# A linear-attention and MoE kernel: queries projected with tokens moving, and their maxima taken across partitions

## The chip, the cores and the metric

The kernel runs on one core of a Trainium2 chip. The time is device microseconds of one launch; three runs of the kernel before gave 825.32, 826.61 and 826.67 us, median 826.61.

## What is computed

```python
def phi(x):
    proj = np.einsum('bhsd,df->bhsf', x, w_phi)
    proj = proj - np.max(np.abs(proj), axis=-1, keepdims=True)
    return np.concatenate([np.exp(proj), np.exp(-proj)], axis=-1)
q_p, k_p = (phi(q), phi(k))
kv = np.einsum('bhsf,bhsd->bhfd', k_p, v)
z = np.sum(k_p, axis=2)
num = np.einsum('bhsf,bhfd->bhsd', q_p, kv)
den = np.einsum('bhsf,bhf->bhs', q_p, z)[..., None] + 1e-06
attn = num / den
```

There are 8 batches, 8 heads, 576 tokens, a head dimension of 64 and 128 features. The heads' outputs are laid side by side (512 wide) and go through h = relu(x @ w_in) (1024 wide), a convolution over three neighbouring tokens, a sigmoid gate of it on h, and a product with w_out. All is fp32 in and out.

## The kernel before, in words

**Products in parts.** Most operands are split into a high part that TensorE takes in its fp32r format and the rest, a low part, and three products (high by high, high by low, low by high) are summed. `split` (L57) does this with a copy and a subtraction. Batch 0's queries, and a few other products, are plain fp32 and take one instruction, of which the trace shows two records.

**Attention.** A unit is one batch `b` and one half `qd` of its heads, 16 units in all. Of a unit, group 0 holds 128 token columns (the last 64 tokens of two head pairs) and groups 1 to 4 hold 256 tokens of one pair. A tile's two heads lie on partitions 0 to 63 and 64 to 127. So there are 80 groups of queries, 64 large and 16 small, and as many of keys.

`load_split` (L172) loads a group by SyncE's queue and splits it on GpSimd (L62, L65). `project` (L185) makes, for each 128 tokens, a product with the tokens as the stationary operand and a block-diagonal `w_phi` of 256 columns moving: the result has tokens on partitions and features along the row (L196 in fp32, or L199 to L201). VectorE takes each row's maximum (L204) and subtracts it (L206), from PSUM to SBUF. Keys stay so. In `q_process` (L300) each 128 x 128 block of the queries is then transposed by TensorE with an identity matrix (L320, tile tp), ScalarE makes both exponentials (L326), splits them with VectorE (tile ql), and the products with kv (L348, L356, tile nm) follow. kv's own products (L255) are interleaved with them. `x_process` (L384) divides: sums go by DMA to one row (den, L392, L393, rr), VectorE multiplies (L406) and, with ScalarE, splits the result into xh and xl. xl1_3_0 is batch 1, head pair 3, half 0 of the tokens.

**MoE.** For each batch and each half of its tokens (16 parts, n = 2 b + half) `h_part` makes h (L429, tile hp), GpSimd and VectorE convolve (L452, L457, tile c), ScalarE's sigmoid gates, VectorE multiplies (L465) and splits (tile gl), and `o_part` makes the output (L488, tile op). hp2 is the first part of batch 1. `weight_process` rounds the 16 pieces of the MoE weights at the start (tiles w_t and w_r, L96 to L105), on VectorE, ScalarE and GpSimd.

**The order.** The program is written out by a planner (L513 on): each process yields estimates of TensorE's time (`pe(ns)`), delays (`wait(ns)`) and conditions (`until`), up to 13 attention processes are open at once, and attention and MoE are interleaved by their remaining shares. A scheduler then sets each engine's queue. Engines run their queues in that order. The lines around the change:

```python
pr = project(n, hi, lo, b, qd, g, "q")
yield pe(330 * n)
...
tp = pg.tile([P, 2, n, P], F32, name=f"tp{b}_{qd}_{g}", tag="g", bufs=4)
for t in range(n):
    for i in range(2):
        nc.tensor.transpose(out=tp[:, i, t, :], in_=pr[:, 2 * t + i, :], identity=idn)
```

Four PSUM buffers (tag g) serve the key and query projections, the transposes and nm.

## Time and profile before

| what | value |
|---|---|
| median of three runs | 826.61 us |
| the profiled execution | 825.6 us |
| its span, first to last instruction | 823.5 us |
| mean granted TensorE clock | 0.989 |
| busy share of ScalarE, GpSimd | 69%, 37% |
| first matmul of the MoE (hp0) | at 65.7 us |
| hp2, the MoE's first part of batch 1 | at 210.0 us |
| attention's last query group | ends near 708 us |

The profile's views give, for a group of like instructions, their count, their busy time, the mean of one, and the engine's idle time just before them with what ended it. PE is TensorE's matmuls, PEld its weight loads, DVE VectorE, ACT ScalarE, POOL GpSimd, SP SyncE. Matmuls are pipelined, so one's duration is longer than the time from its start to the next one's.

### The profile page before, as it was taken

What the parts mean: (1) busy time and instruction counts of PE and PEld (TensorE: products, weight loads), DVE (VectorE), ACT (ScalarE), POOL (GpSimd) and SP (SyncE); (2) the same over time, 40 slices, a digit from 0 to 9 for tenths busy, and PEclk for the clock granted to TensorE, in tenths of its full rate; (3) what the DMA queues carried; (4) which work ended last, traced back from release to release, by engine and by line L of the source; (5) the groups of instructions that cost most, each with busy time, mean ns of one, the idle gap of its engine ahead of it and who ended that gap; (6) DMA issues with size and microseconds to landing.
All of it is one profiled execution on the core that took longest, in us unless ns stands there. A gap on an engine that the chain in (4) does not pass through costs nothing.

```text
span 823.5 us, 17817 instructions
## 1 busy us (share of the span) xinstructions
PE 788.0 (96%) x6350; PEld 772.5 (94%) x6350; DVE 645.6 (78%) x1390; ACT 569.5 (69%) x1228; POOL 307.6 (37%) x467
## 2 busy tenths in 40 slices
PE   7778779999999999999999999999999999999998
PEld 6767678999999999999999999999999999999998
DVE  4879999799987769787779878788697878766551
ACT  4598777797788867687586857678576867644332
POOL 4757765444443424414233333424334131111110
PEclk9799989999999999999999999999999999999999
DMA  6544421211211302121121211112021100000001
GB/s 187 157 134 135 135 66 47 67 41 44 70 56 44 93 18 71 27 82 50 46 61 43 69 34 60 47 50 82 15 77 29 56 12 19 13 30 30 23 23 44
DMA packets 56328, 49.18 MB, mean 60 GB/s; under 512 B 15024, under 2 KB 54192, under 8 KB 56240
## 3 DMA queue, kind: packets, MB, share of 16 engines
q1 hardware_dynamic: 56240, 48.05, 20.1%
q8 instruction: 51, 0.84, 0.4%
q14 instruction: 37, 0.30, 0.1%
HBM read 38.13 MB, written 9.44 MB: 58 GB/s over the span
## 4 chain that ended last, share of the span: by engine, by line
PE 74%; DVE 10%; ACT 7%; issue 4%; DMA 3%; POOL 1%; SPq 1%; DVEq 0%; ACTq 0%; POOLq 0%
PE op L488 22%; PE hp L429 21%; PE kv L255 8%; PE nm L356 8%; PE tp L320 3%; PE kp L199 2%; PE nm L348 2%; PE kp L200 2%; PE kp L201 2%; PE qp L199 1%; PE qp L200 1%; PE qp L201 1%; DMA w_r<-in_w_in_dram 1%; PE kv L251 1%; DVE qm L204 1%
## 5 line engine op out<-in xcount | busy, mean ns | idle before, releaser
L457 DVE SCALAR_TENSOR_TENSOR c<-h,cw,c 128x287 f32<-128x287 f32 (+1 forms) x256 | 138.7, 554 | 49.4 <-POOL c L452 47.5
L452 POOL TENSOR_SCALAR c<-h,cw 128x288 f32<-128x288 f32 x128 | 75.0, 588 | 243.6 <-ACT h L436 184.3
L255 PE MATMUL kv<-v,ke 128*128 128x65 f32 x1024 | 159.4, 255 | 1.4 <-ACT ke L236 1.2
L255 PEld LDWEIGHTS kv<-v,ke 128*128 128x128 f32 x1024 | 153.5, 193 | 4.8 <-ACT ke L236 1.8
L429 PE MATMUL hp<-xh,win_hi 128*128 128x290 f32 x512 | 153.2, 300 | 0.6 <-ACT os L493 0.6
L429 PE MATMUL hp<-xl,win_hi 128*128 128x290 f32 x512 | 152.7, 298 | 0.2 <-DVE xl L65 0.2
L488 PE MATMUL op<-gh,wout_hi 128*128 128x288 f32 x512 | 152.2, 298 | 0.0
L429 PE MATMUL hp<-xh,win_lo 128*128 128x290 f32 x512 | 151.9, 297 | 0.0
L488 PE MATMUL op<-gl,wout_hi 128*128 128x288 f32 x512 | 151.4, 296 | 0.0
L488 PE MATMUL op<-gh,wout_lo 128*128 128x288 f32 x512 | 150.9, 295 | 0.0
L436 ACT ACTIVATE h<-hp 128x290 f32<-128x290 f32 x128 | 52.2, 414 | 71.7 <-PE hp L429 71.2
L429 PEld LDWEIGHTS hp<-xh,win_hi 128*128 128x128 f32 x512 | 96.7, 190 | 1.5 <-ACT os L493 1.4
L62 POOL TENSOR_SCALAR kxh<-kr 128x256 fp32r<-128x256 f32 (+1 forms) x80 | 43.8, 547 | 144.1 <-PE kp L200 134.6
L429 PEld LDWEIGHTS hp<-xl,win_hi 128*128 128x128 f32 x512 | 97.0, 189 | 0.6 <-DVE xl L65 0.6
L429 PEld LDWEIGHTS hp<-xh,win_lo 128*128 128x128 f32 x512 | 97.1, 190 | 0.0
L488 PEld LDWEIGHTS op<-gh,wout_lo 128*128 128x128 f32 x512 | 96.4, 188 | 0.0
L488 PEld LDWEIGHTS op<-gl,wout_hi 128*128 128x128 f32 x512 | 96.2, 188 | 0.0
L488 PEld LDWEIGHTS op<-gh,wout_hi 128*128 128x128 f32 x512 | 96.1, 188 | 0.0
L65 DVE TENSOR_TENSOR ql<-qe,qh 128x512 fp32r<-128x512 f32 x112 | 79.9, 732 | 9.9 <-ACT qh L60 9.5
L236 ACT ACTIVATE ke<-ks 128x512 f32<-128x512 f32 (+1 forms) x80 | 46.9, 586 | 39.1 <-DVE ks L206 36.5
L326 ACT ACTIVATE qe<-tp 128x512 f32<-128x512 f32 x112 | 61.2, 595 | 12.2 <-PE tp L320 10.4
L356 PE MATMUL nm<-ql,kvh 128*65 128x256 f32 x224 | 68.4, 308 | 0.3 <-DVE ql L65 0.2
(84 smaller groups left out, 1989.5 us busy)
## 6 DMA issues: line engine op xcount, KB each, us to landing
v<-in_vt_dram SPq DMA_DIRECT2D x80, 130.0 KB
out_dram<-os SPq DMA_DIRECT2D x64, 144.0 KB
qr<-in_qT_dram SPq DMA_DIRECT2D x64, 128.0 KB
kr<-in_kT_dram SPq DMA_DIRECT2D x64, 128.0 KB
w_r<-in_w_in_dram SPq DMA_DIRECT2D x8, 512.0 KB
w_r<-in_w_out_dram SPq DMA_DIRECT2D x8, 512.0 KB
rr<-rc SPq DMA_DIRECT2D x128, 2.2 KB
qr<-in_qT_dram SPq DMA_DIRECT2D x16, 64.0 KB
```

The lines of the kernel that those rows point to most:

```text
L62: nc.gpsimd.tensor_scalar(out=hi, in0=src, scalar1=1.0, scalar2=0.0, op0=ALU.mult, op1=ALU.add)
L65: eng_lo.tensor_tensor(out=lo, in0=src, in1=hi.bitcast(F32), op=ALU.subtract)
L199: nc.tensor.matmul(out=o, lhsT=his, rhs=wbd_hi, start=True, stop=False)
L236: nc.scalar.activation(out=e[:, 0], in_=pr, func=AF.Exp)
L255: ins = nc.tensor.matmul(out=kp[i][:, s, p0 : p0 + VW], lhsT=lhsT, rhs=v[:, (2 * t + i) * VW : (2 * t + i + 1) * VW], start=False, stop=(g ...
L326: nc.scalar.activation(out=e, in_=tp.rearrange("p i t s -> p i (t s)"), func=AF.Exp, scale=1.0 - 2.0 * s)
L356: ins = after(ins, lambda: nc.tensor.matmul(out=ps[:, i, o : o + w], lhsT=w_, rhs=x_, start=(k == 0), stop=(k == 5)))
L429: nc.tensor.matmul(out=ps, lhsT=w_, rhs=x_, start=(k == 0), stop=(k == 11))
L436: nc.scalar.activation(out=hs, in_=ps, func=AF.Relu)
L452: nc.gpsimd.tensor_scalar(out=cv, in0=hs[:, o : o + TC], scalar1=cw[:, f, 1:2], scalar2=0.0, op0=ALU.mult, op1=ALU.add)
L457: nc.vector.scalar_tensor_tensor(out=cv[:, lo:hi], in0=hs[:, o + j - 1 + lo : o + j - 1 + hi], scalar=cw[:, f, j : j + 1], in1=cv[:, lo:hi ...
L488: nc.tensor.matmul(out=ps, lhsT=w_, rhs=x_, start=(k == 0), stop=(k == 23))
```

## The change

The queries' projection is turned round. The weights (64 x 128, the same for both heads) are stationary and the tokens move, 512 columns for two heads of 256 tokens, so that features come out on partitions as the exponentials need them.

- Loading: the two heads lie side by side along the row, and the same data is loaded twice, to partitions 0 to 63 and 64 to 127 (two DMAs instead of one, except in batch 0). GpSimd splits the whole (a copy on 128 partitions x 512, then a subtraction on the upper 64), so that the upper half holds the low parts.
- Two matmuls of 512 columns make the projection: `wq_hi` (the high weights, in both halves) and `wq_lo` (the low weights, zero below). In batch 0 one fp32 product on 64 partitions does it.
- The maximum over features now runs across partitions. VectorE's reduce with `apply_transpose` takes it in blocks of 32 partitions x 32 columns, three copies bring the other quarters' maxima to partitions 64 to 95, and a second small reduce joins them.
- GpSimd splits the maxima in two parts (two small ops) and multiplies them with a 32 x 32 identity (`eye`) into the moving operand's upper half, which is free by then.
- A third matmul, with -1 as its weights (`wq_m`), subtracts the maximum into the same PSUM buffer, and the exponentials read that.
- The subtraction on VectorE (L206) and the transposes are gone for queries, so are the PSUM buffer tp and the 128 x 128 identity. The planner's estimates follow (`pe(230 * n)`, `pe(115 * n)`). Keys stay as they are.

```diff
+        if kind == "q":
+            f32 = 2 * b + qd < NQ_F32
+            raw = sb.tile([P, 2, n * P], F32, name=f"qr{b}_{qd}_{g}", tag="qr", bufs=2)
+            for h in range(1 if f32 else 2):
+                nc.sync.dma_start(out=raw[D * h : D * h + D, :, :],
+                                  in_=src[b, qd, :, c0 : c0 + n * P].rearrange("(i d) s -> d i s", d=D))
+            x = sb.tile([P, 2, n * P], F32R, name=f"qx{b}_{qd}_{g}", tag="qx", bufs=2)
+            if f32:
+                return n, x, raw
+            nc.gpsimd.tensor_scalar(out=x, in0=raw, scalar1=1.0, scalar2=0.0, op0=ALU.mult, op1=ALU.add)
+            nc.gpsimd.tensor_tensor(out=x[D:P], in0=raw[D:P], in1=x[D:P].bitcast(F32), op=ALU.subtract)
+            return n, x, None
...
-        pr = project(n, hi, lo, b, qd, g, "q")
-        yield pe(330 * n)
-        yield wait(1700)
+        if raw is None:
+            nc.tensor.matmul(out=tpf, lhsT=wq_hi, rhs=xf, start=True, stop=False, skip_group_check=True)
+            nc.tensor.matmul(out=tpf, lhsT=wq_lo, rhs=xf, start=False, stop=False, skip_group_check=True)
+        else:
+            nc.tensor.matmul(out=tpf, lhsT=wbd_f[0:D, 0:F], rhs=raw.rearrange("p i s -> p (i s)")[0:D], start=True, stop=False,
+                             skip_group_check=True)
+
+        c = w // 32
+        mt = sb.tile([P, 4, 16], F32, name=f"qmt{b}_{qd}_{g}", tag="qmt", bufs=2)
+        nc.vector.tensor_reduce(out=mt[:, 2, 0:c], in_=tpf.rearrange("p (c f) -> p c f", f=32), axis=AX, op=ALU.max,
+                                apply_absolute_value=True, apply_transpose=True)
+        for a in (0, 1, 3):
+            nc.vector.tensor_copy(out=mt[D : D + 32, a, 0:c], in_=mt[32 * a : 32 * a + 32, 2, 0:c])
+        m = sb.tile([P, 16], F32, name=f"qm{b}_{qd}_{g}", tag="qm", bufs=2)
+        nc.vector.tensor_reduce(out=m[D : D + 32, 0:c], in_=mt[D : D + 32, :, 0:c].rearrange("p a c -> p c a"), axis=AX, op=ALU.max)
+        mp = sb.tile([P, 16], F32R, name=f"qmp{b}_{qd}_{g}", tag="qmp", bufs=2)
+        nc.gpsimd.tensor_copy(out=mp[D : D + 32, 0:c], in_=m[D : D + 32, 0:c])
+        nc.gpsimd.tensor_tensor(out=mp[D + 32 : P, 0:c], in0=m[D : D + 32, 0:c], in1=mp[D : D + 32, 0:c].bitcast(F32),
+                                op=ALU.subtract)
+
+        nc.gpsimd.tensor_tensor(out=xf[D:P, :].rearrange("p (c t) -> p c t", t=32),
+                                in0=mp[D:P, 0:c].bitcast(F32).unsqueeze(2).broadcast_to([D, c, 32]),
+                                in1=eye[D:P, :].unsqueeze(1).broadcast_to([D, c, 32]), op=ALU.mult)
+        yield pe(230 * n)
+        yield wait(2500)
...
-        for t in range(n):
-            for i in range(2):
-                nc.tensor.transpose(out=tp[:, i, t, :], in_=pr[:, 2 * t + i, :], identity=idn)
+        r = slice(0, P) if raw is None else slice(D, P)
+        nc.tensor.matmul(out=tpf, lhsT=wq_m[r, :], rhs=xf[r, :], start=False, stop=True, skip_group_check=True)
...
-        yield pe(220 * n)
+        yield pe(115 * n)
```

The planner and the scheduler make a new order of it. Line numbers in the rows of the order of the changed kernel are its own: L335, L336 and L362 are the three matmuls, L338 the fp32 product, L343, L346 and L348 the reduce, the copies and the second reduce, L197, L198, L350, L351 and L354 GpSimd's five ops, L471 and L530 hp and op. Names carry batch, half and group, and a running number of the tile.

On TensorE, just ahead of hp2, before:

```order
L199 MATMUL qp2_1_1_2878<-wbd_hi_72,qxh2_1_1_2738 128x256
L200 MATMUL qp2_1_1_2878<-wbd_lo_73,qxh2_1_1_2738 128x256
L201 MATMUL qp2_1_1_2878<-wbd_hi_72,qxl2_1_1_2739 128x256
...
L488 MATMUL op0_3_2409<-gl0_4_2222,wout_hi7_108 128x288
L488 MATMUL op0_3_2409<-gh0_4_2221,wout_lo7_116 128x288
L429 MATMUL hp2_0_2938<-xh1_0_0_2001,win_hi0_93 128x290
```

and now:

```order
L335 MATMUL qp2_0_1_2545<-qx2_0_1_2317,wq_hi_76 128x512
L336 MATMUL qp2_0_1_2545<-qx2_0_1_2317,wq_lo_77 128x512
L530 MATMUL op0_3_2445<-gh0_4_2271,wout_lo7_126 128x288
L471 MATMUL hp2_0_2964<-xh1_0_0_2048,win_hi0_103 128x290
L471 MATMUL hp2_0_2964<-xl1_0_0_2049,win_hi0_103 128x290
```

The projections are two long matmuls instead of six, and when hp2 is reached the queries stand at group 1 of unit (2, 0), not of unit (2, 1): less attention stands ahead of it.

On VectorE, around xl1_3_0, before:

```order
L465 TENSOR_TENSOR c1_2231<-c1_2231,h1_6_2100 128x288
L465 TENSOR_TENSOR c1_2231<-c1_2231,h1_7_2115 128x288
L65 TENSOR_TENSOR xl1_3_0_2857<-xf1_3_0_2853,xh1_3_0_2856 128x290
L204 TENSOR_REDUCE km2_1_4_2812<-kp2_1_4_2805 128x4
L65 TENSOR_TENSOR xl1_3_1_2864<-xf1_3_1_2860,xh1_3_1_2863 128x290
L204 TENSOR_REDUCE qm2_1_0_2823<-qp2_1_0_2819 128x2
```

and now:

```order
L447 STREAM_SHUFFLE xf1_3_1_2920<-rr_84 128x290
L448 TENSOR_TENSOR xf1_3_0_2913<-num1_1_1_1978,xf1_3_0_2913 128x290
L448 TENSOR_TENSOR xf1_3_1_2920<-num1_1_1_1978,xf1_3_1_2920 128x290
L65 TENSOR_TENSOR ql2_0_2_2663<-qe2_0_2_0_2664,qh2_0_2_2662 128x512
L65 TENSOR_TENSOR xl1_3_0_2917<-xf1_3_0_2913,xh1_3_0_2916 128x290
L65 TENSOR_TENSOR ql2_0_2_2663<-qe2_0_2_1_2668,qh2_0_2_2662 128x512
L65 TENSOR_TENSOR xl1_3_1_2924<-xf1_3_1_2920,xh1_3_1_2923 128x290
L343 TENSOR_REDUCE qmt2_0_3_2689<-qp2_0_3_2686 128x16
L346 COPY qmt2_0_3_2689<-qmt2_0_3_2689 32x16 x3
L348 TENSOR_REDUCE qm2_0_3_2694<-qmt2_0_3_2689 32x16
```

A query group's reduce and subtraction are now a reduce, three copies and a small reduce. Ahead of xl1_3_0 stand 23 query groups, and stood 25; all 16 pieces gl of the MoE's first two parts stand ahead of it now, and 8 did.

On GpSimd, in batch 1, the changed kernel has:

```order
L350 CAST qmp1_1_2_1630<-qm1_1_2_1628 32x16
L351 TENSOR_TENSOR qmp1_1_2_1630<-qm1_1_2_1628,qmp1_1_2_1630 32x16
L354 TENSOR_TENSOR qx1_1_2_1482<-qmp1_1_2_1630,eye_81 64x512
L197 TENSOR_SCALAR qx1_1_4_1651<-qr1_1_4_1648 128x512
L198 TENSOR_TENSOR qx1_1_4_1651<-qr1_1_4_1648,qx1_1_4_1651 64x512
L494 TENSOR_SCALAR c1_2281<-h1_0_1787,cw_92 128x288
L494 TENSOR_SCALAR c1_2281<-h1_2_1817,cw_92 128x288
...
L350 CAST qmp1_1_3_1907<-qm1_1_3_1905 32x16
L494 TENSOR_SCALAR c1_2281<-h1_6_2156,cw_92 128x288
```

Where only the splits of loaded queries and keys stood between the convolution's ops, the middle step of a query group now stands there too, behind the convolution's ops that wait for h.

More of the change, by code (lines that the diff above doesn't have):

```diff
@@ L78 @@
     split(wbd_f, wbd_hi, wbd_lo, nc.vector, nc.vector)
-    idn = load_const(ident, [P, P], "idn")
+    wq_hi = cp.tile([P, F], F32R, name="wq_hi")
+    wq_lo = cp.tile([P, F], F32R, name="wq_lo")
+    wq_m = cp.tile([P, F], F32R, name="wq_m")
+    for i in range(2):
+        r = slice(D * i, D * i + D)
+        nc.vector.tensor_copy(out=wq_hi[r, :], in_=wbd_hi[r, i * F : (i + 1) * F].bitcast(F32))
+    eye = cp.tile([P, 32], F32, name="eye")
+    for p in (D, D + 32):
+        nc.sync.dma_start(out=eye[p : p + 32, :], in_=ident[p : p + 32, p : p + 32])
     rr = cp.tile([P, S], F32, name="rr")
     nc.gpsimd.memset(rr, 0.0)
+    nc.gpsimd.tensor_copy(out=wq_m, in_=rr[:, 0:F])
+    nc.gpsimd.tensor_copy(out=wq_lo, in_=rr[:, 0:F])
+    nc.vector.tensor_copy(out=wq_lo[0:D, :], in_=wbd_lo[0:D, 0:F].bitcast(F32))
+    nc.gpsimd.tensor_scalar(out=wq_m[D:P, :], in0=rr[D:P, 0:F], scalar1=-1.0, scalar2=0.0, op0=ALU.add, op1=ALU.add)
     bias_e = cp.tile([P, 1], F32, name="bias_e")
@@ L173, in load_split @@
         c0, n = group_columns(g)
-        if kind == "q" and 2 * b + qd < NQ_F32:
-            raw = sb.tile([P, n * P], F32, name=f"{kind}r{b}_{qd}_{g}", tag=kind + "xh", bufs=2)
-            nc.sync.dma_start(out=raw, in_=src[b, qd, :, c0 : c0 + n * P])
-            return n, raw, None
+        if kind == "q":
[10 more added lines that the diff above has]
+            return n, x, None
         raw = sb.tile([P, n * P], F32, name=f"{kind}r{b}_{qd}_{g}", tag=kind + "r", bufs=2)
@@ L194, in project @@
             his = hi[:, t * P : (t + 1) * P]
-            if lo is None:
-                nc.tensor.matmul(out=o, lhsT=his, rhs=wbd_f, start=True, stop=True)
-                continue
             los = lo[:, t * P : (t + 1) * P]
@@ L306, in q_process @@
         yield until(back("qp", 2))
-        n, hi, lo = load_split(qT, b, qd, g, "q")
+        n, x, raw = load_split(qT, b, qd, g, "q")
         yield wait(3000)
@@ L310, in q_process @@
         set_ready(("qp", *divmod(j, 5)))
-        pr = project(n, hi, lo, b, qd, g, "q")
-        yield pe(330 * n)
-        yield wait(1700)
+        w = n * 2 * P
+        tp = pg.tile([P, 2, n, P], F32, name=f"qp{b}_{qd}_{g}", tag="g", bufs=4)
+        tpf = tp.rearrange("p i t s -> p (i t s)")
+        xf = x.rearrange("p i s -> p (i s)")
+        if raw is None:
[4 more added lines that the diff above has]
+                             skip_group_check=True)
@@ L314, in q_process @@
+        yield pe(230 * n)
+        yield wait(2500)
         yield until(back("num", 2))
         set_ready(("tp", *divmod(j, 5)))
-        tp = pg.tile([P, 2, n, P], F32, name=f"tp{b}_{qd}_{g}", tag="g", bufs=4)
-        for t in range(n):
-            for i in range(2):
-                nc.tensor.transpose(out=tp[:, i, t, :], in_=pr[:, 2 * t + i, :], identity=idn)
+        r = slice(0, P) if raw is None else slice(D, P)
+        nc.tensor.matmul(out=tpf, lhsT=wq_m[r, :], rhs=xf[r, :], start=False, stop=True, skip_group_check=True)
```

## The prediction

> **What bounds the kernel now.** The page's busy shares come first, then the stretches, then the meeting point of two engines.
>
> ```profile
> span 823.5 us, 17817 instructions
> PE 788.0 (96%) x6350; PEld 772.5 (94%) x6350; DVE 645.6 (78%) x1390; ACT 569.5 (69%) x1228; POOL 307.6 (37%) x467
> ```
>
> TensorE looks like the bound, but that is a mean. The stretches (length, then busy time of PE, PEld, DVE, ACT, POOL) show two different kernels:
>
> ```profile
> 0.00:60.00 60.00, 45.69 (x293) 40.96 (x294) 41.43 (x76) 37.86 (x78) 34.68 (x47) 0.91 0.53 155
> 60.00:140.00 80.00, 64.88 (x497) 58.54 (x496) 78.45 (x147) 61.94 (x134) 56.61 (x66) 0.96 0.35 104
> 140.00:210.00 70.00, 68.47 (x576) 67.70 (x575) 61.54 (x136) 58.12 (x123) 31.42 (x47) 1.00 0.20 54
> 210.00:700.00 490.00, 489.65 (x4106) 487.52 (x4105) 394.63 (x869) 358.74 (x780) 168.70 (x277) 1.00 0.18 50
> 700.00:823.50 123.50, 119.29 (x888) 117.75 (x886) 69.52 (x167) 52.88 (x116) 16.20 (x32) 1.00 0.08 27
> ```
>
> From 60 to 140 us VectorE is busy 78.45 of 80 us and TensorE only 64.88: VectorE paces that part (it also converts the MoE weights there). From 140 us on TensorE is full, VectorE at 81% (394.63 of 490). The hand-over is batch 1's input to the MoE: its piece xl1_3_0 is made by VectorE here, and TensorE starts the MoE part hp2, which reads it, here.
>
> ```profile
> 206.22 0.45 DVE L65 TENSOR_TENSOR xl<-xf,xh 128x290 fp32r<-128x290 f32 x1
> 209.99 0.30 PE L429 MATMUL hp<-xh,win_hi 128*128 128x290 f32 x1
> ```
>
> Every engine runs its queue in order, so the time is: the start of hp2 (210.0), plus TensorE's work queued from there on, plus what it idles after.
>
> **TensorE's part of the change.** Matmuls overlap, so I price them from start to start:
>
> ```profile
> 208.35 0.28 PE L199 MATMUL qp<-wbd_hi,qxh 128*128 128x256 f32 x1
> 209.06 0.30 PE L488 MATMUL op<-gh,wout_lo 128*128 128x288 f32 x1
> 716.18 12.80 PE op L488 x96
> 80.80 0.60 PE L320 MATMUL tp<-idn,qs 128*128 128x128 f32 x4
> 41.77 1.56 PE L196 MATMUL qp<-wbd_f,qr 128*128 128x256 f32 x6 [1.18 <-ACT qh L326]
> 56.31 1.13 PE L196 MATMUL qp<-wbd_f,qr 128*128 128x256 f32 x4 [1.55 <-ACT qh L326]
> ```
>
> Six q projections of 256 columns lie between the first two starts: 0.71/6 = 0.118 us. 288 columns take 12.80/96 = 0.133, so 32 columns more cost 0.015 and 512 columns, which no row shows, are estimated at 0.225 (0.118 + 256 x 0.42 ns). Four transposes end 0.60 us after the first started; less one's 0.28 of latency that is 0.108 each. Two fp32 records more cost 0.43, so a 256-column fp32 product (two records) is 0.43 and a 512-column one 0.86.
>
> The Trainium skill, "TensorE: Matmul & The Clock Gate", section on 56 against 53.3 ns, states N/2.4 GHz + 2.5 ns, 215.7 ns at 512 columns. By that the 176 matmuls of 512 columns would be 1.6 us cheaper in all; its 109 ns at 256 columns is less than the 118 shown, so I stay with 0.225.
>
> A group of 256 tokens x 2 heads: before 6 x 0.118 + 4 x 0.108 = 1.14, after 3 x 0.225 = 0.675; a 128-token group 0.57 and 0.35; the ten fp32 groups of batch 0 go from 1.30 to 1.09. With 56 and 14 groups of the first kinds the cut is 26.0 + 3.0 + 1.9, about **31 us** of TensorE work. Of these, work ahead of hp2 is worth nothing by itself: at such prices the rows ahead of it fill some 155 of the 210 us.
>
> What counts stands behind hp2. Counting the rows of the order: before, 288 q matmuls (34.0) and 198 transposes (21.4) stand behind it, 55.4 us; after, 142 of 512 and 33 of 256 columns, 35.9 us: 19.5 less. But the new order runs less attention ahead: 27 k projections, 47 products nm of 256 and 8 of 64 columns, 32 + 4 kv products now stand behind hp2 and stood ahead. One nm and two kv records take 0.29 here:
>
> ```profile
> 420.64 0.33 PE L255 MATMUL kv<-v,ke 128*128 128x65 f32 x2
> 420.79 0.31 PE L356 MATMUL nm<-ql,kvh 128*65 128x256 f32 x1
> 420.93 0.33 PE L255 MATMUL kv<-v,ke 128*128 128x65 f32 x2
> ```
>
> So a kv product is 0.17 (the wider ones, and nm of 64 columns, taken in proportion, 0.22 and 0.12): 3.2 + 5.5 + 0.9 + 5.4 + 0.9 = 15.9 us come back. Behind hp2 TensorE has **about 4 us less** to do, not 31. In all there stand behind it, before: 1440 op and 1344 hp (0.133, 0.134), 1095 matmuls of 256 columns, 198 transposes, 328 + 40 kv products, 88 short nm: 597 us; after, 593.5.
>
> **VectorE up to xl1_3_0.** The rows of the first 210 us:
>
> ```profile
> L65 DVE TENSOR_TENSOR ql<-qe,qh 128x512 fp32r<-128x512 f32 x24 | 19.9, 852 | 2.0 <-ACT qh L60 2.0
> L206 DVE TENSOR_TENSOR qs<-qp,qm 128x512 f32<-128x512 f32 x20 | 13.5, 676 | 0.0
> L65 DVE TENSOR_TENSOR xl<-xf,xh 128x290 fp32r<-128x290 f32 x16 | 10.8, 682 | 0.3 <-ACT xh L60 0.3
> L406 DVE TENSOR_TENSOR xf<-num,xf 128x290 f32<-128x290 f32 x16 | 9.7, 636 | 0.0
> L65 DVE TENSOR_TENSOR gl<-c,gh 128x288 fp32r<-128x288 f32 x8 | 3.7, 512 | 0.0
> L392 DVE TENSOR_SCALAR den<-den 72x16 f32<-72x16 f32 x9 | 3.0, 337 | 3.9 <-DMA den<-dr 2.6 <-issue 1.3
> L204 DVE TENSOR_REDUCE qm<-qp 128x2 f32<-128x256 f32 x6 | 2.5, 411 | 0.0
> L392 DVE TENSOR_SCALAR den<-den x32: 156/171/1227, 52.4 to 710.7; 72x16 f32<-72x16 f32 x32
> ```
>
> Ahead of xl1_3_0 stood 25 q groups (5 of them small), each a reduce and a subtraction at 0.676 or 0.411: 31.2 us. Now 23 stand there (5 small). No row has the transposing reduce; I take the plain one's price: 18 x 0.676 + 5 x 0.411 = 14.2. The second reduce over 64 elements is estimated at 0.21 (0.676 less 448 elements at 1.04 ns, the slope between 0.411 and 0.676): 4.8. The other differences, 8 gl more, 3 ql, one k group and one den less, cancel. That is -12 us, and 69 copies of 32x16 come in. Nearest row: the 72x16 op, 0.156 at its fastest, 0.337 on average here. So the sum is **-1 to +11 us**; at 0.26, midway, +6.
>
> These copies read and write SBUF, and GpSimd is a neighbour that hurts: the same ops late in the kernel, where GpSimd is 13% busy (16.20 of 123.5) and not 58% (122.7 of 210), take
>
> ```profile
> L65 DVE TENSOR_TENSOR ql<-qe,qh 128x512 fp32r<-128x512 f32 x3 | 2.1, 688 | 1.0 <-ACT qh L60 1.0
> L65 DVE TENSOR_TENSOR xl<-xf,xh 128x290 fp32r<-128x290 f32 x8 | 3.7, 463 | 1.2 <-ACT xh L60 1.2
> ```
>
> while qs, fed from PSUM, is not stretched. The excess is 0.16 us on a ql of 0.69 and 0.22 on an xl of 0.46. These are the other large ones with SBUF operands up to 210 us; with ql, xl, xf, gl and den they make 111 us, and at a quarter over the free price some 22 of them are excess:
>
> ```profile
> L103 DVE SCALAR_TENSOR_TENSOR w_t<-w_t,w_r 128x512 f32<-128x512 int32 x16 | 14.8, 922 | 0.0
> L100 DVE SCALAR_TENSOR_TENSOR w_t<-w_r,w_t 128x512 int32<-128x512 int32 x16 | 12.4, 777 | 0.0
> L98 DVE TENSOR_SCALAR w_t<-w_r 128x512 int32<-128x512 int32 x16 | 9.6, 602 | 6.5 <-ACT w_t L97 6.5
> L457 DVE SCALAR_TENSOR_TENSOR c<-h,cw,c 128x288 f32<-128x288 f32 x16 | 9.2, 599 | 0.0
> L457 DVE SCALAR_TENSOR_TENSOR c<-h,cw,c 128x287 f32<-128x287 f32 x16 | 9.1, 584 | 1.0 <-POOL c L452 1.0
> L96 DVE TENSOR_SCALAR w_t<-w_r 128x512 int32<-128x512 int32 x16 | 8.6, 539 | 2.0 <-DMA w_r<-in_w_in_dram 1.0 <-POOL wout_lo L65 0.8
> ```
>
> **GpSimd gets the new work.** Rows of the first 210 us, and the one small op:
>
> ```profile
> L105 POOL TENSOR_TENSOR w_t<-w_t 128x512 f32<-128x512 f32 x16 | 22.0, 1373 | 10.0 <-DVE w_t L103 7.4 <-DVE den L392 2.6
> L65 POOL TENSOR_TENSOR qxl<-qr,qxh 128x256 fp32r<-128x256 f32 x15 | 13.4, 902 | 0.3
> L62 POOL TENSOR_SCALAR qxh<-qr 128x256 fp32r<-128x256 f32 x15 | 6.9, 465 | 12.8 <-PE qp L200 12.8
> L105 POOL TENSOR_TENSOR cw<-cw,cw_power 128x24 f32<-128x24 f32 x1 | 0.2, 237 | 1.3 <-DVE cw L103 1.3
> ```
>
> A group's split was 0.465 + 0.902 = 1.37. Now: split 2 x 0.465 + 1.37, two small ops 0.47, product 1.37: 4.1 us (64 partitions taken as dear as 128). An fp32 group goes from nothing to 1.8. To xl1_3_0 this adds 10 x 2.75 + 8 x 1.85 + some 6 for the small groups, 48 us: GpSimd from 58% to about 78% busy. If the 22 us of excess on VectorE grow in proportion, by a third, and the copies share in it, that is +8 us. VectorE idled 10 us from 60 to 210; I let it win 4 of them back. So hp2 starts at 210 + 6 + 8 - 4 = **220 us**.
>
> **The rest.** After hp2 the old kernel lost 823.5 - 210.0 - 597 = 16.5 us. With 57 groups left VectorE gets about 10 us of small ops, and with GpSimd at some 60% the excess that the first part shows: 88 ql at 0.16, 48 xl and 48 xf at 0.2 are 33 us, part of which is there already, and with the 288-column ops I take 35: 440 of some 485 us, 91%. Each third matmul also waits in TensorE's queue for a chain of 0.68 + 3 copies + 0.21 + 0.47 + 1.37, some 3.5 us, where 8 us of other matmuls stand between at the median of all groups, 4 at the least, by the order and the prices above; the MoE's matmuls queue behind it. I add 5 us of idle. Lower bound 0; upper 25, if VectorE can be kept only at the 86% of the first 210 us (440/0.86 = 512).
>
> Sum: 220 + 593.5 + 21.5 = 835.0 of span, + 2.1 around it (825.6 for 823.5) = 837 against 825.6; the median of the runs, 826.6, stands 1.0 above the profiled execution: **838 us**.
>
> **Rivals.**
> *VectorE keeps pace* (0.29): copies at 0.156, neighbours no dearer, 8 us of idle won back: hp2 at 201, then 593.5 + 16.5: 811 + 3 = 814 us. For it: 140 to 210 us, where TensorE's relief can speed VectorE (61.54 of 70). Against: 78.45 of 80 before. For all 31 us to show (796), hp2 would have to come at 183; VectorE's busy time before 210 alone is 181, so that is the edge of this case.
> *The shared path of VectorE and GpSimd is the bound* (0.12). VectorE's 111 us with SBUF operands and GpSimd's 122.7 make 234 in 210; after, 111 + 69 x 0.26 = 129 and 171 make 300. Did they exclude each other throughout, hp2 would move in proportion, to 269: 882 us. The Trainium skill, "SBUF — State Buffer", section "Who interferes with whom", has this rule: an exclusive lock, the loser blocks for the whole instruction. The stretched ql and xl agree in kind; from 60 to 140 us both engines are nevertheless busy together for at least 55 us, part of it with PSUM-fed ops.
> *The transposing reduce runs at half rate* (0.09): 1.2 us for 512 elements adds 11 us up to xl1_3_0 and 28 behind it, 468 of VectorE's time; kept at 90%, those are 520 us: 231 + 520 + 123.5 + 3, some 877 us.
>
> **The numbers.** A difference of 0.2% is about what measurements of this kernel can tell. My forecast has 0.50, likeliest range 816 to 856, of which 0.06 lies within 0.2% and 0.04 below. Faster: 0.29 + 0.04 = 0.33; slower: 0.40 + 0.12 + 0.09 = 0.61. The range 803 to 866 leaves out the edge of the first rival and most of the other two.
>
> **What would show it.** Right: hp2 starts after 212 us; VectorE near full from 60 to 210; GpSimd above 70% there; ql and xl longer; the copies 0.15 to 0.35 us. Wrong: hp2 before 205, or TensorE stalls on third matmuls adding over 25 us after hp2, or a transposing reduce far from 0.68 us.

## The result and the profile after

The changed kernel takes **930.0 us** (median of four runs, 923.8 to 936.3) against 826.6 us before: 1.1255 times as long, with a 95% interval of 1.1154 to 1.1357. The prediction had 838 and a range up to 866. Slower was right; the size is missed by 92 us. The profiled execution is the longest of the four, 936.25 us, so its parts add up to about 6 us more than the median.

The page of the changed kernel, with its busy times, the granted clock in 40 slices and the chain that ended last:

```profile
span 934.5 us, 17563 instructions
PE 824.8 (88%) x5888; PEld 774.8 (83%) x5888; DVE 758.6 (81%) x1633; ACT 574.9 (62%) x1228; POOL 503.0 (54%) x710
PEclk9988778999799998999989899799999999999999
PE 38%; DVE 32%; ACT 10%; POOL 9%; issue 7%; DMA 3%; SPq 1%; POOLq 0%; DVEq 0%; ACTq 0%
```

Before, the same chain read

```profile
PE 74%; DVE 10%; ACT 7%; issue 4%; DMA 3%; POOL 1%; SPq 1%; DVEq 0%; ACTq 0%; POOLq 0%
```

TensorE held three quarters of the path and now holds 38%; VectorE's part went from 10% to 32%. VectorE is 113 us busier (645.6 to 758.6) and GpSimd 195 us (307.6 to 503.0). The stretches of the changed kernel (length, then busy time of PE, PEld, DVE, ACT, POOL, then the clock):

```profile
0.00:60.00 60.00, 54.22 (x242) 43.54 (x242) 38.71 (x81) 29.56 (x60) 32.83 (x57) 1.00 0.45 127
60.00:140.00 80.00, 54.45 (x282) 42.59 (x283) 71.81 (x135) 49.17 (x101) 63.47 (x72) 0.77 0.36 105
140.00:210.00 70.00, 61.94 (x439) 58.70 (x437) 66.89 (x128) 44.38 (x98) 49.76 (x61) 0.90 0.20 55
210.00:700.00 490.00, 430.65 (x3257) 411.38 (x3257) 417.53 (x916) 322.65 (x690) 283.12 (x410) 0.95 0.21 59
```

From 210 to 700 us TensorE was full before (489.65 of 490) and is now busy 430.65, at a granted clock of 0.95: it has holes, and part of its work runs at half speed (from 245 to 248 us the granted clock is 0.50, and products of 256 columns start 0.21 us apart in place of 0.12). So it no longer sets the pace there. The hand-over of the prediction has come apart into two moments. Matmuls of hp2, and the piece xl1_3_0 that most of them still need:

```profile
223.97 0.29 PE L471 MATMUL hp<-xh,win_hi 128*128 128x290 f32 x1
...
234.69 0.40 PE L471 MATMUL hp<-xl,win_hi 128*128 128x290 f32 x1 [2.47 <-DVE xl L65]
...
251.52 0.30 PE L471 MATMUL hp<-xh,win_hi 128*128 128x290 f32 x1
```
```profile
247.44 0.45 DVE L65 TENSOR_TENSOR xl<-xf,xh 128x290 fp32r<-128x290 f32 x1
```

hp2 starts at 224.0, but gets only 18 matmuls done on the pieces that are there; xl1_3_0 is made at 247.4 to 247.9 and the rest of hp2 runs from 251.5. Before, the piece came at 206.2 and hp2 started behind it, at 210.0.

VectorE's rows over the whole span, first before, then after, show where its 113 us come from:

```profile
L65 DVE TENSOR_TENSOR ql<-qe,qh 128x512 fp32r<-128x512 f32 x112 | 79.9, 732 | 9.9 <-ACT qh L60 9.5
L206 DVE TENSOR_TENSOR ks<-kp,km 128x512 f32<-128x512 f32 x64 | 43.6, 681 | 0.8
L65 DVE TENSOR_TENSOR xl<-xf,xh 128x290 fp32r<-128x290 f32 x64 | 34.4, 552 | 8.8 <-ACT xh L60 8.8
L406 DVE TENSOR_TENSOR xf<-num,xf 128x290 f32<-128x290 f32 x64 | 32.0, 522 | 0.0
L65 DVE TENSOR_TENSOR kvl<-kvf,kvh 128x260 fp32r<-128x260 f32 x28 | 12.3, 449 | 0.1
```
```profile
L65 DVE TENSOR_TENSOR ql<-qe,qh 128x512 fp32r<-128x512 f32 x112 | 91.6, 828 | 16.1 <-ACT qh L60 15.4
L343 DVE TRANSPOSE_TENSOR_REDUCE qmt<-qp 128x16 f32<-128x512 f32 x64 | 45.1, 705 | 6.8 <-PE qp L338 4.3 <-PE qp L336 2.2
L346 DVE COPY qmt<-qmt 32x16 f32<-32x16 f32 x192 | 43.9, 228 | 3.7
L225 DVE TENSOR_TENSOR ks<-kp,km 128x512 f32<-128x512 f32 x64 | 43.3, 680 | 0.6
L448 DVE TENSOR_TENSOR xf<-num,xf 128x290 f32<-128x290 f32 x64 | 40.5, 652 | 0.2
L65 DVE TENSOR_TENSOR xl<-xf,xh 128x290 fp32r<-128x290 f32 x64 | 39.7, 634 | 1.1 <-ACT xh L60 0.8
L65 DVE TENSOR_TENSOR kvl<-kvf,kvh 128x260 fp32r<-128x260 f32 x28 | 16.5, 604 | 0.1
L348 DVE TENSOR_REDUCE qm<-qmt 32x16 f32<-32x64 f32 x64 | 16.2, 254 | 2.8
```

The new operations cost what was estimated: the transposing reduce 705 ns (0.68), the second reduce 254 (0.21), the copies 228 (0.26). With the small groups they are 125 us, and 99 us of old reduces and subtractions went: a net of 26. The other 87 us lie on operations that nobody changed: 76 of them are longer times in the rows, and successive operations also overlap less. Operations with two inputs in SBUF are longer by an eighth to a third (ql 732 to 828, xl 552 to 634, xf 522 to 652, kvl 449 to 604, the convolution's c 554 to 636) and make about 60 of the 76; the rest is mostly on operations with one input in SBUF (kvh, a cast, 293 to 484; den 260 to 459). ks, which reads PSUM, is not longer (681 and 680), and neither is the shuffle of xf (484 and 483), though it reads SBUF. GpSimd's new and changed rows:

```profile
L198 POOL TENSOR_TENSOR qx<-qr,qx 64x512 fp32r<-64x512 f32 x56 | 82.9, 1482 | 4.5
L354 POOL TENSOR_TENSOR qx<-qmp,eye 64x512 fp32r<-64x512 f32 x64 | 75.2, 1176 | 4.6 <-PE qp L362 0.3
L197 POOL TENSOR_SCALAR qx<-qr 128x512 fp32r<-128x512 f32 x56 | 40.9, 730 | 13.6 <-PE qp L362 11.7
L350 POOL CAST qmp<-qm 32x16 fp32r<-32x16 f32 x64 | 23.5, 368 | 160.4 <-DVE qm L348 160.0
```

The first three are long steps on SBUF. The last shows a wait that the change added, on VectorE's maxima, and the list of waits has its other end, TensorE waiting for the product:

```profile
POOL qmp L350 <- DVE qm L348: 178.4, 65, 11.2
PEld qp L362 <- POOL qx L354: 27.4, 27, 4.3
PE qp L362 <- POOL qx L354: 21.5, 21, 4.1
```

Two explanations offer themselves. One is a round trip: TensorE, VectorE, GpSimd, TensorE, each step in a queue in order, so that TensorE stands (**Loop**). The other is load: GpSimd's added work on SBUF stretches VectorE, VectorE becomes the pace, and the waits are only where that shows (**Load**).

### The profile page after: what moved, and what is told of

It reads as the page before. It is cut to its first block, busy times and chain, and to the rows that moved or that the text cites. A ratio compares the mean times of both kernels' runs of the same rounds, so it can differ in the third digit from the quotient of the medians.

```text
span 934.5 us, 17563 instructions
## 1 busy us (share of the span) xinstructions
PE 824.8 (88%) x5888; PEld 774.8 (83%) x5888; DVE 758.6 (81%) x1633; ACT 574.9 (62%) x1228; POOL 503.0 (54%) x710
## 4 chain that ended last, share of the span: by engine, by line
PE 38%; DVE 32%; ACT 10%; POOL 9%; issue 7%; DMA 3%; SPq 1%; POOLq 0%; DVEq 0%; ACTq 0%
PE hp L471 11%; PE op L530 11%; DVE c L499 7%; PE kv L274 5%; PE nm L398 4%; DVE ql L65 3%; DVE qmt L346 3%; DVE xl L65 2%; DVE xf L448 2%; DVE qmt L343 2%; DVE c L507 2%; POOL qx L354 2%; DVE xf L447 2%; DVE gl L65 2%; DVE ks L225 2%
## 5 line engine op out<-in xcount | busy, mean ns | idle before, releaser
L499 DVE SCALAR_TENSOR_TENSOR c<-h,cw,c 128x287 f32<-128x287 f32 (+1 forms) x256 | 160.1, 636 | 49.3 <-POOL c L494 46.4
L274 PEld LDWEIGHTS kv<-v,ke 128*128 128x128 f32 x1024 | 165.9, 206 | 7.1 <-issue 1.9
L274 PE MATMUL kv<-v,ke 128*128 128x65 f32 x1024 | 169.6, 266 | 0.0
L530 PE MATMUL op<-gh,wout_hi 128*128 128x288 f32 x512 | 156.2, 305 | 6.7 <-ACT os L535 4.9
L471 PE MATMUL hp<-xl,win_hi 128*128 128x290 f32 x512 | 155.1, 303 | 6.5 <-DVE xl L65 6.5
L471 PE MATMUL hp<-xh,win_hi 128*128 128x290 f32 x512 | 155.7, 305 | 5.3 <-ACT os L535 2.3
L530 PE MATMUL op<-gh,wout_lo 128*128 128x288 f32 x512 | 155.2, 303 | 0.0
L530 PE MATMUL op<-gl,wout_hi 128*128 128x288 f32 x512 | 155.0, 303 | 0.0
L471 PE MATMUL hp<-xh,win_lo 128*128 128x290 f32 x512 | 154.4, 302 | 0.0
L350 POOL CAST qmp<-qm 32x16 fp32r<-32x16 f32 (+1 forms) x80 | 29.1, 365 | 179.1 <-DVE qm L348 178.4
L530 PEld LDWEIGHTS op<-gh,wout_hi 128*128 128x128 f32 x512 | 99.7, 195 | 8.3 <-ACT os L535 6.0
L471 PEld LDWEIGHTS hp<-xh,win_hi 128*128 128x128 f32 x512 | 98.8, 193 | 8.5 <-ACT os L535 3.1
L471 PEld LDWEIGHTS hp<-xl,win_hi 128*128 128x128 f32 x512 | 99.0, 193 | 8.0 <-DVE xl L65 7.5
L65 DVE TENSOR_TENSOR ql<-qe,qh 128x512 fp32r<-128x512 f32 x112 | 91.6, 828 | 16.1 <-ACT qh L60 15.4
L530 PEld LDWEIGHTS op<-gl,wout_hi 128*128 128x128 f32 x512 | 99.9, 195 | 0.5
L530 PEld LDWEIGHTS op<-gh,wout_lo 128*128 128x128 f32 x512 | 99.9, 195 | 0.4
L471 PEld LDWEIGHTS hp<-xh,win_lo 128*128 128x128 f32 x512 | 99.0, 193 | 0.3
L198 POOL TENSOR_TENSOR qx<-qr,qx 64x512 fp32r<-64x512 f32 (+1 forms) x70 | 94.2, 1347 | 5.5
L354 POOL TENSOR_TENSOR qx<-qmp,eye 64x512 fp32r<-64x512 f32 (+1 forms) x80 | 86.1, 1079 | 6.2 <-DMA eye<-in_ident_dram 0.5
```

The source lines that it names most:

```text
L65: eng_lo.tensor_tensor(out=lo, in0=src, in1=hi.bitcast(F32), op=ALU.subtract)
L198: nc.gpsimd.tensor_tensor(out=x[D:P], in0=raw[D:P], in1=x[D:P].bitcast(F32), op=ALU.subtract)
L274: ins = nc.tensor.matmul(out=kp[i][:, s, p0 : p0 + VW], lhsT=lhsT, rhs=v[:, (2 * t + i) * VW : (2 * t + i + 1) * VW], start=False, stop=(g ...
L350: nc.gpsimd.tensor_copy(out=mp[D : D + 32, 0:c], in_=m[D : D + 32, 0:c])
L354: nc.gpsimd.tensor_tensor(out=xf[D:P, :].rearrange("p (c t) -> p c t", t=32), in0=mp[D:P, 0:c].bitcast(F32).unsqueeze(2).broadcast_to([D, ...
L471: nc.tensor.matmul(out=ps, lhsT=w_, rhs=x_, start=(k == 0), stop=(k == 11))
```

## The experiments

Times are medians. The kernel before took 825.3 to 826.2 us beside them. Runs of the changed kernel and its variants spread by 1 to 1.5%, so differences below some 8 us between two variants decide nothing, and the medians of x1 and x2, of two runs each, are the least certain.

**x1, the round trip cut.** GpSimd's two small operations read a constant tile in place of the maxima; VectorE still makes the maxima, and the shift of the queries is wrong.

```
-        nc.gpsimd.tensor_copy(out=mp[D : D + 32, 0:c], in_=m[D : D + 32, 0:c])
+        nc.gpsimd.tensor_copy(out=mp[D : D + 32, 0:c], in_=mc[D : D + 32, 0:c])
```

> The changed kernel, with GpSimd's two small ops reading a constant tile in place of the maxima that VectorE makes (so a constant is subtracted and not the maximum; every instruction and its size stays). Loop theory (the new round trip TensorE, VectorE, GpSimd, TensorE through queues kept in order costs the time; GpSimd waited 178 us for qm): under 870 us. Load theory (GpSimd's added work stretches VectorE's ops with SBUF operands, and VectorE paces the kernel): 900 to 935 us, with ql at 0.8 us and more as now.

921.0 us (914.0 and 927.9), 9 below the changed kernel; the lowest runs of the two are 10 apart. ql takes 806 ns. The 178 us of GpSimd's wait for VectorE are gone from its list, and the time is nearly not. (The product still waits for the first two passes, which read the rows that it overwrites.) Loop, in which the wait for the maxima makes the loss, falls.

**x2, GpSimd's product on one block of 32 columns** outside batch 0; the other columns keep what the split left there.

```
-        nc.gpsimd.tensor_tensor(out=xf[D:P, :].rearrange("p (c t) -> p c t", t=32), ...
+            nc.gpsimd.tensor_tensor(out=xf[D:P, 0:32], ...
```

> The changed kernel, with GpSimd's product made on one block of 32 columns instead of 16 (8) outside batch 0, so the maximum is not subtracted rightly; the chain and its waits stay, some 1 us shorter a group, and GpSimd loses about 65 us of work. Loop theory: 895 to 925 us. Load theory: the excess on VectorE falls by about a quarter, 880 to 895 us.

902.1 us (895.2 and 909.0): 28 us for 60 us less of GpSimd's work (503.0 to 443.5). Inside the one range, 7 us above the other: it leans to neither.

**x3, the kernel before with GpSimd's load alone.** Products that nobody reads, at the places where the changed kernel has its new steps; nothing waits for them.

```
+            nc.gpsimd.tensor_tensor(out=dv[D:P, 0:k], in0=wbd_f[D:P, 0:k], in1=wbd_f[D:P, 0:k], op=ALU.mult)
...
+        for o in (0, D):
+            nc.gpsimd.tensor_tensor(out=dv[o : o + 32, 0:16], ...
+        for _ in range(2):
+            nc.gpsimd.tensor_tensor(out=dv[D:P, 0:k], ...
```

> The kernel before, with GpSimd ops added that nobody waits for and that wait for nothing: one 64x256 product for each query group outside batch 0 where it is loaded, and two small products and two 64x256 products for each query group where it is projected, about 190 us of GpSimd work in all, as much as the change added. Loop theory: 826 to 840 us. Load theory: 880 to 930 us, with ql, xl and xf as long as in the changed kernel (0.83, 0.63, 0.65 us).

898.4 us, 1.0888 times before (1.0856 to 1.0919). No query step was touched and no chain added: 73 us come from work on GpSimd alone. The time is Load's. The durations are not: ql took 789 ns, xl 586 and xf 539, each between before and the changed kernel and xf close to before. So this load alone does not make all of the changed kernel's stretch.

**x4, the changed kernel without GpSimd's middle step and without the third pass.** VectorE makes the maxima and nobody reads them; the queries are not shifted.

```
-        nc.gpsimd.tensor_tensor(out=xf[D:P, :].rearrange("p (c t) -> p c t", t=32), ...
-        nc.tensor.matmul(out=tpf, lhsT=wq_m[r, :], rhs=xf[r, :], start=False, stop=True, skip_group_check=True)
```

> The changed kernel without GpSimd's small ops and product and without the third matmul: the exponentials take the projection with no maximum subtracted; VectorE still makes the maxima, and the larger splits stay. Loop theory: 800 to 835 us, the loop is gone and the rest of TensorE's cut shows. Load theory: GpSimd keeps some 90 us of the added work, so VectorE stays stretched by half: 850 to 880 us.

856.0 us, 1.0374 (1.0344 to 1.0404): 74 us back, but still 30 above before, with 47 us less of TensorE work than before by the prediction's prices (31 and the third passes, 16). From 210 to 700 us VectorE is busy 443.07 and TensorE 455.42:

```profile
210.00:700.00 490.00, 455.42 (x3597) 441.54 (x3596) 443.07 (x1004) 358.55 (x765) 212.61 (x277) 0.98 0.22 64
```

Load was then split in two for x5, x6 and x12: **Port**, in which instructions of GpSimd that read SBUF and VectorE's with two SBUF operands hold each other up, and **Queue**, in which GpSimd is simply late with its own queue, whatever it runs.

**x5, the middle step on VectorE** in place of GpSimd, nothing left out; four `nc.gpsimd` became `nc.vector`.

> The changed kernel with GpSimd's middle step (the two small ops and the product with the identity) made by VectorE: GpSimd loses about 118 us, VectorE gains about 0.16 + 0.16 + 0.68 us a group, 75 us. Port theory: VectorE is what paces, and most of the added ops have two SBUF operands: 900 to 930 us. Queue theory: the round trip to GpSimd and its late queue are gone: 860 to 885 us.

929.5 us, 1.1263 (1.1220 to 1.1306), as the changed kernel: Port's range, not Queue's. GpSimd is down to 369.6 us, VectorE up to 813.1 (88% of the span). Whoever of the two does the work, the pair pays.

**x6, the kernel before with fills.** As x3, but the added work only writes: `memset`, two ahead of a projection and seven behind it.

```
+        for _ in range(7):
+            nc.gpsimd.memset(dv[:, 0:k], 0.5)
```

> The kernel before, with GpSimd fills of a scratch tile added that nobody waits for: two for each query group outside batch 0 where it is loaded, seven for each where it is projected, some 190 us in all as in the run with added products, but they only write and read nothing. Port theory (GpSimd's reads of SBUF and VectorE's ops with two SBUF operands hold each other up): 826 to 850 us, ql near 0.73 us. Queue theory (GpSimd's own queue comes late with splits and convolutions, whatever it runs): 880 to 905 us, as with the products.

839.7 us, 1.0175 (1.0143 to 1.0208). The load is like that of x3, but somewhat smaller: the fills add 184 us to GpSimd's busy time, the products 223. Here the pages of the two and their first 210 us, x3 first:

```profile
PE 818.2 (91%) x6350; PEld 793.9 (89%) x6350; DVE 687.9 (77%) x1390; ACT 573.3 (64%) x1228; POOL 530.4 (59%) x857
0.00:210.00 210.00, 170.09 (x1154) 156.28 (x1155) 167.04 (x309) 137.45 (x295) 186.57 (x308) 0.87 0.32 94
L65 DVE TENSOR_TENSOR ql<-qe,qh 128x512 fp32r<-128x512 f32 x112 | 86.6, 789 | 15.5 <-ACT qh L60 15.3
```
```profile
PE 796.9 (95%) x6350; PEld 777.4 (93%) x6350; DVE 660.4 (79%) x1390; ACT 571.1 (68%) x1228; POOL 491.5 (59%) x1167
0.00:210.00 210.00, 179.36 (x1313) 165.53 (x1314) 187.14 (x347) 152.65 (x321) 179.19 (x398) 0.93 0.34 99
L65 DVE TENSOR_TENSOR ql<-qe,qh 128x512 fp32r<-128x512 f32 x112 | 80.6, 737 | 16.3 <-ACT qh L60 16.0
```

GpSimd is 59% busy in both, and about 180 of the first 210 us. With products ql takes 789 ns and the kernel 73 us more; with fills ql takes 737 (before 732) and the kernel 14 us more. kvl shows it most (591 and 435 ns), xl less (586 and 526), xf not at all (539 in both). The 39 us by which the loads differ would be worth some 13 at x3's 0.33 us for one, not 59. So it isn't that GpSimd is full; it is that its instructions read SBUF. Port, not Queue.

**x7, the kernel before with 80 more reduces on VectorE**, fed from PSUM.

```
+            nc.vector.tensor_reduce(out=m2, in_=ps3, axis=AX, op=ALU.max, apply_absolute_value=True)
```

> The kernel before, with the reduce of the query groups made a second time behind the subtraction (result unused): 80 reduces from PSUM, 50 us of VectorE in all, that GpSimd doesn't touch. If VectorE's time is what the kernel has no room for: 850 to 875 us, half of the 50 us or more coming through. If it has room and only GpSimd matters: 826 to 838 us.

848.4 us, 1.0280 (1.0248 to 1.0312): VectorE is 37 us busier, the kernel 23 us slower, between the two expectations. The old kernel's VectorE has some room, not much.

For the next runs the rival is **Frame**: the new order of the program, and the PSUM buffer that a query group now holds through its third pass, cost by themselves, whatever the two engines do.

**x8, the changed kernel without the three copies**; the second reduce takes one block of 32 features, so the maxima are not the right ones.

```
-        for a in (0, 1, 3):
-            nc.vector.tensor_copy(out=mt[D : D + 32, a, 0:c], in_=mt[32 * a : 32 * a + 32, 2, 0:c])
```

> The changed kernel without the three copies across partitions: the second reduce takes the maxima of one block of 32 features only, so the maxima are not the right ones; GpSimd, TensorE and every other instruction stay. VectorE loses some 54 us of small ops. Load (VectorE's and GpSimd's added work costs, VectorE's own at the 0.45 us for 1 us that the 80 extra reduces showed): 895 to 918. Frame (the new order of the program and the PSUM buffer held through the third pass cost by themselves, whatever the two engines do): 920 to 935.

874.5 us, 1.0616 (1.0550 to 1.0682): 55 us back for 60 us of VectorE's work, more than Load had said. In the changed kernel these copies count nearly one for one; they also stand in the chain from the projection to the third pass, which is shorter without them. Frame is out for this part.

**x9, the rounded copy of the queries on ScalarE** in place of GpSimd, nothing left out.

```
-            nc.gpsimd.tensor_scalar(out=x, in0=raw, scalar1=1.0, scalar2=0.0, op0=ALU.mult, op1=ALU.add)
+            nc.scalar.activation(out=x, in_=raw, func=AF.Copy)
```

> The changed kernel with the rounded copy of the queries made by ScalarE in place of GpSimd, nothing left out: GpSimd loses 41 us, ScalarE gains some 35. Load (GpSimd's added work at the 0.38 us for 1 us that the extra products showed): 905 to 922. Frame: 922 to 935.

904.4 us, 1.0936 (1.0898 to 1.0974): 26 us back for 46 us less on GpSimd (503.0 to 457.3), just under Load's range (905) and well below Frame's; it is also a better version of the change, and still far above before.

**x12, all queries in one fp32 product** (`NQ_F32 = 16`), nothing left out: no split, one load, and a dearer first pass.

> The changed kernel with all batches' queries projected as batch 0's are (one fp32 product on 64 partitions, no split, one load): GpSimd loses the splits, some 143 us; TensorE gets about 0.4 us a large group more, 26 us; the middle step stays. Port theory: VectorE's excess falls by a third, 865 to 890 us. Queue theory: 845 to 870 us. If neither load matters: 940 us and more.

892.5 us, 1.0814 (1.0642 to 1.0987), a little above Port's range. TensorE has more to do and the kernel is 38 us faster than the changed one, with GpSimd at 362.4 us.

**x10, no maxima at all**, on top of x4: VectorE has neither reduces nor copies for the queries, which are not shifted. **x16** is the same with 300 in place of 2500 for the planner's wait ahead of the exponentials. **x13** is x10 without the subtraction that makes the queries' low part on GpSimd.

```
-        nc.vector.tensor_reduce(out=mt[:, 2, 0:c], ...
...
-            nc.gpsimd.tensor_tensor(out=x[D:P], in0=raw[D:P], in1=x[D:P].bitcast(F32), op=ALU.subtract)
```

> The changed kernel without any maximum: no reduces, no copies, no work of GpSimd between, no third pass; the queries are not shifted. The two projection passes, the split of the queries on GpSimd, the order of the rest and the buffers stay. VectorE has some 75 us less than the kernel before, GpSimd some 50 us more, TensorE some 40 less. Load: 795 to 825, as VectorE has room again. Frame: above 830.

> The kernel without maxima and third pass (839 us) with 300 in place of 2500 between the second pass and the exponentials, which now follow at once: same instructions, other order, the PSUM buffer given back sooner in the plan. Frame: 800 to 825. Load: 830 to 848.

> The changed kernel without any maximum and third pass, and also without the subtraction that makes the low part of the queries on GpSimd (the second half of the rows stays as copied): GpSimd loses 91 us against the kernel without maxima (839 us) and has some 30 less than before. TensorE's work, VectorE's instructions and the planner's costs stay. Load (GpSimd's work at 0.4 to 0.5 us for 1 us): 792 to 808. Frame (the order and the buffers cost by themselves): 828 to 840.

x10 took 839.2 us, 1.0159 (1.0100 to 1.0218): **against Load as I had put it**, which said 795 to 825. VectorE is lighter than before the change (613.3 us), TensorE has 47 us less to do, and the kernel is slower than before. That left either GpSimd's split or the order of the program. x16 took 830.7, 1.0050 (1.0015 to 1.0085): another order is worth some 8 us, which is Load's range and not Frame's. x13 took **806.1 us, 0.9726 (0.9655 to 0.9796)**, faster than before: one subtraction on GpSimd, 91 us of it, was worth 33. (The projection then also waits for one step less.) x13 still loads the queries twice, so the second load isn't what costs. The pages of x10 and x13, and their ql:

```profile
PE 778.0 (92%) x5808; PEld 743.5 (88%) x5808; DVE 613.3 (73%) x1233; ACT 577.1 (69%) x1228; POOL 365.9 (43%) x470
L65 DVE TENSOR_TENSOR ql<-qe,qh 128x512 fp32r<-128x512 f32 x112 | 88.4, 799 | 30.3 <-ACT qh L60 29.9
```
```profile
PE 752.3 (94%) x5808; PEld 723.4 (91%) x5808; DVE 566.0 (71%) x1233; ACT 571.3 (72%) x1226; POOL 275.7 (35%) x400
L65 DVE TENSOR_TENSOR ql<-qe,qh 128x512 fp32r<-128x512 f32 x112 | 81.7, 734 | 41.9 <-ACT qh L60 41.4
```

VectorE runs the same 1233 instructions in 613.3 and in 566.0 us. The 47 us between them are stretch.

**x11, the load of x3 cut** to a bit over half (one product behind the projection in place of two, and only in three of five groups).

> The kernel before with about 60% of the independent GpSimd products that cost 73 us (the same small ones, the same one ahead of the projection, about a third of the ones behind it). Load in proportion: 860 to 880. If GpSimd costs only once it runs short of room near the start: below 850. If the small ones alone cost: above 885.

865.7 us, 1.0479 (1.0454 to 1.0504). GpSimd has 133 us more than before (440.9) and the kernel 39; in x3 it is 223 and 73. So it goes about in proportion, 0.30 and 0.33 us for one.

**x14 and x15, other orders of the changed kernel**, nothing left out: the planner's old costs for the query step, and 6000 in place of 2500 between the second and the third pass.

> The changed kernel with the planner's old costs for the query step (330, 1700 and 220 in place of 230, 2500 and 115), so the same instructions in another order; nothing left out. If the order makes the loss: at least 15 away from 930. Load: 918 to 942.

> The changed kernel with the planner told that 6000 and not 2500 pass between the second and the third pass, so that more of other work stands between them in every queue; nothing left out. If TensorE's waits on the third pass make the loss (some 60 us of idle and the clock that they cost): 860 to 900. Load: 915 to 945, since what does not wait there waits elsewhere.

925.8 us (1.1184, 1.1107 to 1.1261) and 922.3 us (1.1140, 1.1102 to 1.1177): the first within the spread of the changed kernel's runs, the second 1.5 us below their lowest. In x15 TensorE still waits 23.3 us for the product. Neither of these orders takes back more than 8 of the 104 us; x16's change of order, too, was worth 8.

**x17, the changed kernel with fills**, which puts Port and Queue to the changed kernel itself. GpSimd's two long steps, the subtraction and the product, each became two fills of the same rows with zeros; so the queries' low part and the shift are left out, while place and waits stay, and most of the time on GpSimd.

```
-            nc.gpsimd.tensor_tensor(out=x[D:P], in0=raw[D:P], in1=x[D:P].bitcast(F32), op=ALU.subtract)
+            for _ in range(2):
+                nc.gpsimd.memset(x[D:P].bitcast(F32), 0.0)
```

> The changed kernel with GpSimd's two long steps, the subtraction of the split and the product, each replaced by two fills of the same rows with zeros (0.58 us each by the one fill of 576 columns, so 1.16 us a step, where the two steps take 1.29 and 1.05 at their fastest): their place, their waits and about their time stay, but they read nothing; the queries' low part and the subtraction of the maxima are left out of the result. Shared path (GpSimd's reads hold up VectorE's operations on SBUF, and those hold up GpSimd): 850 to 880, ql below 760 ns. Own lateness (a long step on GpSimd delays the third pass whatever it does): 905 to 930.

871.3 us, 1.0559 (1.0514 to 1.0605): 59 of the 104 us go. Its page, and VectorE's rows that answer to those of the changed kernel:

```profile
PE 797.7 (92%) x5888; PEld 753.5 (87%) x5888; DVE 699.6 (80%) x1633; ACT 575.7 (66%) x1228; POOL 463.1 (53%) x860
L65 DVE TENSOR_TENSOR ql<-qe,qh 128x512 fp32r<-128x512 f32 x112 | 85.7, 767 | 23.7 <-ACT qh L60 23.0
L448 DVE TENSOR_TENSOR xf<-num,xf 128x290 f32<-128x290 f32 x64 | 29.9, 487 | 0.1
L65 DVE TENSOR_TENSOR xl<-xf,xh 128x290 fp32r<-128x290 f32 x64 | 29.6, 481 | 1.8 <-ACT xh L60 1.7
L65 DVE TENSOR_TENSOR kvl<-kvf,kvh 128x260 fp32r<-128x260 f32 x28 | 12.1, 434 | 0.2
```

xf falls from 652 to 487 ns, xl from 634 to 481, kvl from 604 to 434, and VectorE's 1633 instructions from 758.6 to 699.6 us, though GpSimd works at the same places and is busy 53% of the span, against 54%. In us it is 40 less (463.1 against 503.0): two fills take 1.06 us, where the steps had 1.48 and 1.18. At the 0.4 to 0.6 us for one of x2 and x9, 16 to 24 of the 59 us could come from that, and the rest not. ql fell less than I had said (767, not below 760).

## Why the prediction was right in direction and wrong in size

**TensorE's part held.** A product of 512 columns takes 0.23 us from start to start at full clock (223.36 to 223.59 us in the changed kernel), where 0.225 was estimated. With neither maxima nor third pass nor the step for the low part (x13) the kernel falls to 806. No run contradicts the prediction's 721 us of TensorE work for the changed kernel (752 less 31); what grew is the time in which TensorE did not do them, or did them at a lower clock. Span less work was 71.5 us before (823.5 - 752), is 213.5 after (934.5 - 721), and in x10 and x13, with 705 us of work, 137 and 94.

**VectorE up to xl1_3_0: right in its rows, short in its sum.** The new operations cost what was estimated, and GpSimd's 166 us up to that moment are near the 171 foreseen. But VectorE has 33 us more to do by then (212.80 busy to 248 us, where it was 179.42 to 208 before), and I had 14:

```profile
0.00:248.00 248.00, 198.12 (x1147) 169.71 (x1148) 212.80 (x419) 151.96 (x319) 166.15 (x217) 0.88 0.31 89
```
```profile
0.00:208.00 208.00, 177.04 (x1346) 165.21 (x1347) 179.42 (x351) 156.43 (x329) 121.98 (x157) 0.96 0.35 102
```

About 9 of the 33 are the change's own operations, where I had 6: the 69 copies took 0.27 us on average, with 0.26 estimated. The other 24 lie on unchanged operations, 21 of them in their rows' longer times, where I had priced 8, scaled from GpSimd's busy time alone. I also let VectorE win back 4 us of idle; it idles 35 us where it idled 29. So the piece came 41 us later than before (247.4 for 206.2), where I had 10. The start of hp2 itself, at 224.0, looks like a hit and isn't: I had taken its start and the arrival of its last input for one moment, which the new order parts.

**"The rest" is the step that failed:** "I add 5 us of idle", bounds 0 to 25. From the start of hp2 on, TensorE lost 710.5 - 593.5 = 117 us, where I had 21.5. From hp2 to hp12 (the last MoE part in front of the tail), after and before:

```profile
224.00:808.00 584.00, 520.07 (x3929) 497.92 (x3929) 494.34 (x1093) 382.49 (x826) 329.08 (x474) 0.95 0.20 57
```
```profile
210.00:698.00 488.00, 487.65 (x4090) 485.52 (x4089) 392.92 (x865) 356.74 (x774) 168.70 (x277) 1.00 0.18 50
```

I had 440 us for VectorE here; it was 494. Three parts make nearly all of its 101 us more. Some 15 are the net of the query groups. I had written "about 10"; at my own prices (0.21 and three copies at 0.26 in place of a subtraction at 0.676 or 0.411) 57 groups would have made 20. Some 26 are a plain omission: I brought the attention work that no longer runs ahead of hp2 back into TensorE's sum (15.9 us) and not into VectorE's (10 ql, 6 km, 5 ks, 4 each of xf, its shuffle and xl, smaller ones, and three query groups, at their means of before). Some 57 are stretch, where I had 35. And VectorE was kept busy 85% of the stretch (494.34 of 584), about the 86% that I had named as the worst case: the share was within my bounds, the busy time was not. TensorE, no longer the pace, idles 64 us in it, and its clock falls to 0.95 of full, which is another 29 us of its work.

**The rivals.** *VectorE keeps pace* is refuted. *The shared path of VectorE and GpSimd is the bound* (0.12, 882 us) was the nearest, in kind and in size. It isn't the total exclusion that I priced, in which hp2 would have moved to 269; but x3 against x6 shows the path at work with the rest held nearly still. x17 against the change agrees, with GpSimd's work 40 us less, and so does x10 against x13, where the subtraction is gone altogether. *The transposing reduce at half rate* is refuted by its 705 ns.

The rule is in the Trainium skill, "SBUF — State Buffer", section "Who interferes with whom": a VectorE instruction with two SBUF inputs contends with a GpSimd instruction that reads SBUF, and not with one that only writes it. The traces agree in the main: xl and xf, with two SBUF inputs, stretch beside the changed kernel's steps (634 and 652 ns) and not beside the fills of x17 (481 and 487; between x3 and x6 ql, kvl and xl differ, xf does not), and ks, with an input from PSUM, never (676 to 683 in every run). The one-input kvh, den and small copies stretch as well, so two inputs are not the whole of it. I had cited the section for its lock and priced the operations by GpSimd's mean busy share; the instructions on both engines that read SBUF, VectorE's with two inputs first, were what had to be counted.

**What stays open.** Of the 104 us, fills take back 59. The rest, 45, is VectorE's own small operations and the round trip together, as far as the runs show: without the copies 55 come back, without the wait for the maxima 9, and the three don't add up; that each gives VectorE room which the others would have used is likely, not shown. x10 less x13 puts 33 us on the split's subtraction alone. Whether VectorE's reads hold up GpSimd in turn, as Port had it, was not tested apart; GpSimd's unchanged operations took about as long in all as before. That the clock's 29 us would come back by themselves if only the holes were closed was not tried apart.
